# Attention and token/channel mixer on one core: a sixth pair of row tiles as block products, and two products of the last pair issued one slot earlier

## The chip, the cores and the metric

The kernel runs on one core of a Trainium2 chip. The metric is the time of one execution on the device in microseconds. Every engine of the core (PE for matrix products, DVE and POOL for elementwise work, ACT for activation functions, SP for most of the DMA issues) works through its own queue in order and waits on semaphores that the other engines raise.

## The reference

Twelve heads of cosine attention over 448 positions in a batch of 8, followed by a mixer: a two-layer product along the positions (448 to 256 to 448) with a residual, and a two-layer product along the channels (768 to 1536 to 768) with a residual.

```
q_n = q / (norm(q) + 1e-6);  k_n = k / (norm(k) + 1e-6)
attn = softmax(q_n @ k_n^T / tau)          # tau = 0.1
x = (attn @ v), heads side by side         # 8 x 448 x 768
u = x + (relu(x^T @ w_tok1) @ w_tok2)^T
out = u + relu(u @ w_ch1) @ w_ch2
```

Inputs and output are float32. The kernel's matrix products take float16.

## The kernel before, in words

**Slots.** The work is cut into 48 slots, one for each pair of heads of one batch element (6 pairs by 8 elements). The order of the instructions is written out by hand; no scheduler changes it. A slot i of the main loop (lines 1071 to 1134) issues, in this order on PE: three score products (`score`, tiles psS, 448 columns each), the product with V of the slot before (`pv_rest`, `pv`, tiles psO), a first piece of channel work, the last quarter of the scores (`score_rest`, psQ), the second position product of two slots before (`tok2`, psU), more channel work, and the first position product of the slot before (`tok1`, psR). ACT takes the exponential of each score tile; DVE divides the PV result by the row sums (`rec` and `x`, lines 405 and 406) and adds the residual (`u`, line 455). `side(i)` issues what prepares later slots: POOL casts V, squares and scales q and k (lines 242, 264, 316, 324), DVE sums the squares (line 280), ACT and DVE make the inverse norms, SP issues the transposes by DMA and the loads. `ACT_SQ` and `ACT_K` say in which slots ACT does the squares instead of POOL.

**Channel work.** Batch element b has 12 first-layer units (`ch1(b, ct)`: six products of 448 columns, ACT writes the result after a ReLU into the tile gt) and seven half row tiles per two elements in the second layer (`ch2`: 12 products of 384 columns, DVE adds u). gt holds two elements at a time, one for even b and one for odd b, so an element's units may only be written when the row tiles of the element two before have been read. The table `WORK` deals these units out over the slots.

**Pairs of row tiles as block products.** Two row tiles r1, r2 of 128 rows can be computed together with seven block products (Strassen's scheme in Winograd's form) of six matmuls each, where the direct way takes eight such groups. The pairs stand in the list `G`. `sg_sum(1..4)` are the four sums of the input, on POOL, into the three tiles sg0 to sg2; `fast_weights2` made the sums of the weights earlier. `sg_first` (one slot) issues products 1 and 2 (`head`), 6 (`middle`) and 7 (`end`); `sg_second` (another slot) issues 5 and 4 (`head`) and 3 (`end`). DVE adds the parts up into two output tiles `osg` (lines 690 and 696; all of DVE's and POOL's elementwise sums are recorded at line 544). A row tile with m = 3 has 64 rows of one batch element and 64 of the next, so its residual is added in two instructions of 64 rows. `FIRST` and `SECOND` give the slots. In `sg_second`, product 3 adds into the same PSUM tile psZ that product 5 began, so that the tile stays occupied between them.

**PSUM.** There are eight banks: a pool `ps` of two single banks (tag "b") and a pool `ps2` of three double banks (tag "s"). Scores, psQ, psY and psZ take turns in the three of `ps2`; psO, psU, psR, psX and psW in the two of `ps`. A product into a bank waits until the engine that reads the earlier tile there has done so.

**The tail.** Batch elements 6 and 7 are computed after slot 47 with the same seven-product scheme in both layers (`p1` to `p7` for the first, `q1` to `q7` for the second). The sums of the first layer's weights are `fast_weights1(1..4)`: number 1 on POOL (tile s1w), number 2 on DVE (s2w, from s1w), number 4 on POOL (s4w, from s2w), number 3 on DVE (in place in wc1t). `fast_x` are the sums of the first layer's input (t1x to t4x), `fast_g(0, k)` the sums of the second layer's input for the first tail pair (s1g, s2g). `upose` turns the residual stream by PE (psT) for the last two slots.

What sets the order around the change is this loop body and the lines that follow it:

```
            if i == NP_ALL - 1:
                fast_weights1(2, nc.vector)
            side(i)
            if i == NP_ALL - 2:
                cast_v(i + 1)
                fast_weights1(1, nc.gpsimd)
```

Of the kernel before, what the change touches and what calls it, by code (L numbers as in the profile page):

```python
# [7 lines left out]
FP32 = mybir.dt.float32  # L8
# [14 lines left out]
def kernel(  # L23
# [12 lines left out]
    nc = tc.nc  # L36

    B, H, S, E = q.shape
    D = H * E
# [7 lines left out]
    DH = 384  # L47
    NPAIR = H // 2
    NP_ALL = B * NPAIR
# [42 lines left out]
    ps2 = ctx.enter_context(tc.tile_pool(name="ps2", bufs=3, space=bass.MemoryType.PSUM))  # L92
# [442 lines left out]
    def ch2(b, m, n):  # L535
        lo, hi, st = CUTS[n]
        return lambda wide: m_ch2(b, m, lo, hi, st, wide)
# [22 lines left out]
    def fast_weights1(n, eng):  # L560
        s, w = fw["s"], w1part
        out, a, b, op = {1: (s[0], w(1, 0), w(1, 1), ALU.add), 2: (s[1], s[0], w(0, 0), ALU.subtract),
                         3: (w(1, 0), w(0, 0), w(1, 0), ALU.subtract), 4: (s[2], w(0, 1), s[1], ALU.subtract)}[n]
        tt(eng, out if n == 3 else out[:], a[:] if n == 2 else a, b[:] if n == 4 else b, op)
# [52 lines left out]
    def p1(d):  # L617
        bank2("X", d)
        prod1(1, d, px, True)
        nc.scalar.activation(out=etile("e1", d), in_=px[d][:, :, 0:S], func=AF.Copy)  # L620
# [60 lines left out]
    def sg_prod(n, r1, r2, out, start=True):  # L681
        s1, s2, s3 = sgs
        a = {1: lambda: part(*r1, 0), 2: lambda: part(*r1, 1), 3: lambda: s2, 4: lambda: part(*r2, 1),
             5: lambda: s1, 6: lambda: s2, 7: lambda: s3}[n]()
        for j in range(HC):
            nc.tensor.matmul(out[:, 0:DH], a[:, j], fast_w2(n, j), start=(start and j == 0), stop=(j == HC - 1),  # L686
                             skip_group_check=True)

    def sg_add(out, src, other):
        tt(nc.vector, out, src[:, 0:DH], other, ALU.add)  # L690
# [14 lines left out]
    def sg_first(r1, r2):  # L705
        def head():
            st = slot_g[r1] = {}
            st["o"] = [outp.tile([128, D], FP32, name=f"osg_{r[0]}_{r[1]}", tag="ost") for r in (r1, r2)]
            y = st["y"] = ps2.tile([128, 512], FP32, name=f"psY_{r1[0]}_{r1[1]}", tag="s")
            o1 = st["o"][0]  # L710
            sg_prod(1, r1, r2, y)
            sg_add_u(o1[:, 0:DH], y, r1, 0)
            x = ps.tile([128, 512], FP32, name=f"psX_{r1[0]}_{r1[1]}", tag="b")
            sg_prod(2, r1, r2, x)
            sg_add(o1[:, 0:DH], x, o1[:, 0:DH])

        def middle():
            st = slot_g[r1]
            sg_prod(6, r1, r2, st["y"], False)
            sg_add_u(st["o"][0][:, DH:D], st["y"], r1, 1)  # L720

        def end():
            st = slot_g[r1]
            sg_prod(7, r1, r2, st["y"], False)
            for h in (1, 0):
                sg_add_u(st["o"][1][:, DH * h:DH * (h + 1)], st["y"], r2, h)

        return head, middle, end

    def sg_second(r1, r2):  # L730
        def head():
            st = slot_g[r1]
            z = st["z"] = ps2.tile([128, 512], FP32, name=f"psZ_{r1[0]}_{r1[1]}", tag="s")
            o2 = st["o"][1]
            sg_prod(5, r1, r2, z)
            sg_add(o2[:, DH:D], z, o2[:, DH:D])
            w = ps.tile([128, 512], FP32, name=f"psW_{r1[0]}_{r1[1]}", tag="b")
            sg_prod(4, r1, r2, w)
            sg_add(o2[:, 0:DH], w, o2[:, 0:DH])
            if r2[1] < 3:  # L740
                sg_store(r2, o2)
            else:
                for n in range(2):
                    (c, p0, p1), = pieces(384, S)
                    nc.sync.dma_start(out=out[r2[0] - 1 + n].rearrange("(p c) d -> c p d", c=NCH)[c, p0:p1],
                                      in_=o2[64 * n:64 * n + 64])

        def end():
            st = slot_g[r1]
            o1 = st["o"][0]  # L750
            sg_prod(3, r1, r2, st["z"], False)
            sg_add(o1[:, DH:D], st["z"], o1[:, DH:D])
            sg_store(r1, o1)

        return head, end
# [122 lines left out]
    def run(b, lo, hi):  # L878
        return [ch1(b, ct) for ct in range(lo, hi)]

    def halves(b, m):
        return [ch2(b, m, 0), ch2(b, m, 1)]

    G = [((1, 1), (1, 2)), ((2, 1), (2, 2)), ((3, 0), (3, 1)), ((4, 0), (4, 1)), ((4, 2), (5, 3))]
    WORK = {
        7: run(0, 0, 2), 8: run(0, 2, 5), 9: run(0, 5, 7), 10: run(0, 7, 10), 11: run(0, 10, 12),
        12: [ch2(0, 0, 0), ch2(0, 1, 0)], 13: [ch2(0, 2, 0)], 14: [ch2(0, 0, 1), ch2(0, 1, 1)],
        15: [ch2(0, 2, 1)] + run(1, 0, 2), 16: run(1, 2, 6), 17: run(1, 6, 9), 18: run(1, 9, 12),
        19: [ch2(1, 3, 0), ch2(1, 0, 0)], 20: [ch2(1, 3, 1), ch2(1, 0, 1)],
        21: run(2, 0, 3), 22: run(2, 3, 7), 23: run(2, 7, 10), 24: run(2, 10, 11), 25: run(2, 11, 12),  # L890
        26: halves(2, 0), 27: run(3, 0, 3), 28: run(3, 3, 4), 29: run(3, 4, 5),
        30: run(3, 5, 9), 31: run(3, 9, 12), 32: [ch2(3, 3, 0), ch2(3, 2, 0)], 33: [ch2(3, 3, 1), ch2(3, 2, 1)],
        34: run(4, 0, 1), 35: run(4, 1, 2), 36: run(4, 2, 5), 37: run(4, 5, 9), 38: run(4, 9, 12),
        39: run(5, 0, 3), 40: run(5, 3, 5), 41: run(5, 5, 6), 42: run(5, 6, 8), 43: run(5, 8, 10), 44: run(5, 10, 12),
        45: [], 46: [], 47: [],
    }
    FIRST = {24: G[0], 28: G[1], 34: G[2], 41: G[3], 46: G[4]}
    SECOND = {25: G[0], 29: G[1], 35: G[2], 45: G[3], 47: G[4]}
    SUMS = {}

    def sums_at(i, *what):
# [3 lines left out]
    for i in (13, 14, 14, 15, 16, 17, 18, 19, 19, 20, 20, 21):  # L905
        n, m = ws.pop(0)
        sums_at(i, lambda n=n, m=m: fast_weights2(n, m))
    for g, at in zip(G, ((22, 23, 24, 25), (26, 27, 28, 29), (32, 33, 34, 35), (39, 40, 41, 42), (46, 46, 45, 47))):
        for n in (3, 1, 2, 4) if g is G[4] else (1, 2, 3, 4):
            sums_at(at[n - 1], lambda n=n, g=g: sg_sum(n, *g))  # L910
    ACT_K = (14, 19, 20)

    LATE = NP_ALL - 10
    ACT_SQ = range(2 * NPAIR + 1, NP_ALL - 5)
# [1 line left out]
    with tc.manual_schedule():  # L916
# [102 lines left out]
        i = NPAIR  # L1019
# [51 lines left out]
        for i in range(NPAIR + 1, NP_ALL):  # L1071
            b, pj = i // NPAIR, i % NPAIR
            for c in range(KC):
                score(i, c)
                if c == 1 and NPAIR + 2 <= i < NP_ALL - 2:
                    norms(i + 2)
            if i == NPAIR + 1:
                upose(i - 4, 2)
                tok2(i - 2, pe=True)
                pv_wide(i - 1)  # L1080
                upose_act(i - 2)
                x_wide(i - 1)
                sums(i + 2)
            else:
                pv_rest(i - 1)
                pv(i - 1, 0)
                pv(i - 1, 1)
            if i == NP_ALL - 1:
                fast_weights1(2, nc.vector)
            side(i)  # L1090
            if i == NP_ALL - 2:
                cast_v(i + 1)
                fast_weights1(1, nc.gpsimd)
            todo = WORK[i]
            first = sg_first(*FIRST[i]) if i in FIRST else None
            second = sg_second(*SECOND[i]) if i in SECOND else None
            if first or second:
                (first or second)[0]()
            elif todo:
                todo.pop(0)(True)  # L1100
            if old(i):
                score(i, KC)
            else:
                score_rest(i)
            if i in ACT_SQ:
                square(i + 3, 1, act=True)
            if first:
                first[1]()
            if i > NPAIR + 1:
                tok2(i - 2)  # L1110
            if i + 1 < DMA_T0:
                tpose(i + 1)
            if first:
                tok1(i - 1)
                first[2]()
            elif todo and not second:
                todo.pop(0)(True)
            for fn in todo:
                fn(False)
            if second:  # L1120
                second[1]()
            if not first:
                tok1(i - 1)
            if i + 3 < NP_ALL:
                sums(i + 3)
            if i == NP_ALL - 3:
                early.close()
                tail = ctx.enter_context(tc.tile_pool(name="tail", bufs=1, side="right", reuse_waits="tile"))
                tail_tiles()
            if i == NP_ALL - 2:  # L1130
                fast_g(0, 1)
                fast_g(0, 2)
            if i == NP_ALL - 1:
                fast_weights1(4, nc.gpsimd)
        last = NP_ALL - 1
        fw["room"] = {}
        p1(0)
        pv_rest(last)
        pv(last, 0)
        pv(last, 1)  # L1140
# [2 lines left out]
        for k in (3, 4):  # L1143
            fw["t"][k] = xtile(k, "x", [128, HD, S])
        gts["new"] = tail2.tile([128, CT, 512], FP16, name="gt_new")
        fast_weights1(3, nc.vector)
        p1(1)
        fast_x(1, 0, HD)
# [128 lines left out]
```

## Time and profile before

| | us |
|---|---|
| median of 3 runs | 378.64 |
| lowest, highest | 378.26, 380.29 |
| profiled execution | 377.93 |
| its span, first to last instruction | 376.1 |
| PE busy | 360.6 |
| DVE busy | 260.5 |
| ACT busy | 251.5 |
| POOL busy | 293.4 |

The profiled execution's own time is 1.8 us longer than its span, and 0.7 us under the median of the runs. In the profile, a line such as L686 is the line of kernel.py that recorded an instruction; `psY<-tw,sg` names what it writes and reads; an idle time in brackets is that of the engine just before the instruction, with the one that ended it. The granted clock of PE was 0.997 over the span. Slots are cut at the start of the first score product (L363) of each; slot 12 starts at 71.5 us, slot 33 at 213.0, slot 47 at 301.4.

### The profile page before, as it was taken

The numbers are of one execution on the slowest core, as the hardware profiler recorded it, in microseconds if no ns is written. First come the engines' busy times: TensorE is split into PE (matmuls) and PEld (weight loads), VectorE is DVE, ScalarE is ACT, GpSimd is POOL, SyncE is SP. The second block draws the span as 40 slices with busy tenths as digits, with TensorE's granted clock in tenths as the row PEclk, the third lists the DMA queues.
The fourth block names the chain that finished last, engine by engine and source line by source line (L and its number), as shares of the span: only waits on it lengthen the run. The fifth ranks groups of instructions, "written<-read, shape, count | busy, mean of one in ns | idle before, by whom it ended". The sixth has DMA issues, their size and how long they took to land.

```text
span 376.1 us, 10388 instructions
## 1 busy us (share of the span) xinstructions
PE 360.6 (96%) x4060; PEld 236.0 (63%) x4060; DVE 260.5 (69%) x589; ACT 251.5 (67%) x440; POOL 293.4 (78%) x405
## 2 busy tenths in 40 slices
PE   6788999999999999999999999999999969999995
PEld 5566666676666766666666766666666646556663
DVE  7789765776556763875864876646777698786873
ACT  5999887857788597666677755978688434265110
POOL 8899998989989987878766887469989962345753
PEclk9999999999999999999999999999999999999998
DMA  7999999988989798879898979979875713103344
GB/s 200 270 254 197 265 255 205 208 149 163 231 206 198 163 246 173 178 171 237 163 204 187 162 182 214 225 172 182 196 148 124 150 40 99 22 3 91 89 125 126
DMA packets 118224, 64.64 MB, mean 172 GB/s; under 512 B 74272, under 2 KB 114848, under 8 KB 118176
## 3 DMA queue, kind: packets, MB, share of 16 engines
q1 hardware_dynamic: 111984, 58.25, 71.1%
q0 software_dynamic: 5616, 5.21, 8.8%
q8 instruction: 31, 0.51, 0.6%
q10 hardware_dynamic: 576, 0.52, 0.5%
q14 instruction: 17, 0.14, 0.1%
HBM read 43.45 MB, written 11.01 MB: 145 GB/s over the span
## 4 chain that ended last, share of the span: by engine, by line
PE 86%; DVE 5%; ACT 5%; DMA 1%; issue 1%; POOL 0%; SPq 0%; DVEq 0%; ACTq 0%
PE psG L483 22%; PE psO L402 9%; PE psF L500 8%; PE psS L363 8%; PE psU L452 5%; PE psR L438 5%; PE psYo L790 4%; PE psY L686 3%; ACT pt L364 3%; PE psY L598 3%; PE psXo L790 3%; PE psZo L790 3%; PE psZ L686 2%; PE psZ L598 2%; PE psX L598 2%; PE psQ L370 2%
## 5 line engine op out<-in xcount | busy, mean ns | idle before, releaser
L364 ACT ACTIVATE pt<-psS 128x896 f16<-128x896 f32 (+1 forms) x156 | 135.7, 911 | 28.3 <-PE psS L363 28.2
L483 PE MATMUL psG<-ut,wc1t 128*128 128x448 f16 x432 | 90.1, 352 | 0.0
L316 POOL TENSOR_TENSOR kq<-kf,rn 128x384 f16<-128x384 f32 (+1 forms) x43 | 38.0, 885 | 35.0 <-DVE rn L293 34.2
L483 PEld LDWEIGHTS <-wc1t 128*128 128x128 f16 x432 | 40.4, 97 | 32.0
L486 ACT ACTIVATE gt<-psG 128x448 f16<-128x448 f32 x72 | 38.9, 541 | 30.6 <-PE psG L483 30.6
L280 DVE TENSOR_REDUCE ssq<-sq 128x15 f32<-128x960 f32 (+2 forms) x45 | 49.9, 1111 | 2.9 <-ACT sq L262 2.9
L441 DVE TENSOR_SCALAR rt<-psR 128x256 f16<-128x256 f32 x48 | 20.1, 418 | 43.6 <-PE psR L438 43.6
L363 PE MATMUL psS<-qk 64*128 64x448 f16 x312 | 41.2, 354 | 4.4 <-DVE qk L342 3.0
L316 POOL TENSOR_TENSOR kq<-qf,rn 112x512 f16<-112x512 f32 x41 | 42.8, 1044 | 2.8
L455 DVE TENSOR_TENSOR u<-psU,x 128x512 f16<-128x512 f32 x48 | 33.1, 689 | 12.4 <-PE psU L452 11.4
L402 PE MATMUL psO<-vt,pt 128*128 128x65 f16 (+1 forms) x1024 | 39.2, 194 | 0.0
L406 DVE TENSOR_TENSOR x<-psO,rec 128x256 f16<-128x256 f32 x82 | 34.8, 424 | 2.8
L402 PEld LDWEIGHTS <-pt 128*128 128x128 f16 (+1 forms) x1024 | 34.2, 97 | 3.5 <-issue 0.9
L500 PE MATMUL psF<-wc2t,gt 128*128 128x384 f16 x192 | 33.8, 326 | 0.0
L264 POOL TENSOR_TENSOR sq<-kf 128x384 f32<-128x384 f32 (+1 forms) x35 | 30.0, 857 | 0.1
L452 PE MATMUL psU<-rt,w2t 128*128 128x128 f16 x384 | 29.4, 220 | 0.6 <-POOL w2t L211 0.6
L452 PEld LDWEIGHTS <-w2t 128*128 128x128 f16 x384 | 24.8, 98 | 8.0 <-DVE rn L293 0.8
L438 PEld LDWEIGHTS <-w1t 128*128 128x128 f16 x384 | 24.8, 98 | 7.9 <-issue 2.1
L438 PE MATMUL psR<-x,w1t 128*128 128x128 f16 x384 | 29.3, 219 | 0.2 <-DVE u L455 0.2
L371 ACT ACTIVATE pt<-psQ 128x448 f16<-128x448 f32 x36 | 19.6, 544 | 12.3 <-PE psQ L370 12.2
L324 POOL TENSOR_SCALAR kq<-kr,rn 64x64 f16<-64x64 f32 x72 | 22.7, 315 | 3.6
L363 PEld LDWEIGHTS <-qk 64*128 64x128 f16 x312 | 12.6, 94 | 19.0 <-issue 6.3
(164 smaller groups left out, 654.5 us busy)
## 6 DMA issues: line engine op xcount, KB each, us to landing
qf<-in_q_dram SPq DMA_DIRECT2D x43, 224.0 KB, 3.9
vf<-in_v_dram SPq DMA_DIRECT2D x36, 192.0 KB, 3.6
kf<-in_k_dram SPq DMA_DIRECT2D x34, 192.0 KB, 3.7
wc1t<-in_moe_w_ch_dram POOLq DMA_DIRECT2D x4, 576.0 KB, 10.5
wc2t<-in_moe_w_ch_dram POOLq DMA_DIRECT2D x2, 1152.0 KB, 12.7
kf<-in_k_dram SPq DMA_DIRECT2D x9, 224.0 KB, 8.4
vf<-in_v_dram SPq DMA_DIRECT2D x9, 224.0 KB, 8.3
kr<-in_k_dram SPq DMA_DIRECT2D x24, 48.0 KB, 3.6
```

Of the source, the lines that this page charges most:

```text
L280: nc.vector.tensor_reduce(out=st["ssq"][0:n, sl], in_=st["sq"][0:n, sl], axis=AXX.X, op=ALU.add)
L316: eng.tensor_tensor(out=kq[0:p, a, 0:n].rearrange("p c g e -> p g c e"), in0=st["kq"[a]][:].rearrange("p (g c) e -> p g c e", g=2), in1=_b ...
L363: nc.tensor.matmul(psS[:, hh, 0:S], qk[hb, c * n:c * n + 128], qm[hb], start=True, stop=True)
L364: nc.scalar.activation(out=pts[i % 2][0:n, 2 * S * c:2 * S * (c + 1)].rearrange("p (h s) -> p h s", h=2), in_=psS[0:n, :, 0:S], func=AF.Ex ...
L402: nc.tensor.matmul(psO[:, m, 0:E + 1], pts[i % 2][0:n, at:at + 128], vt[0:n, i % HP, nch * hh + c, 0:E + 1], start=(old(i) and c == 0), st ...
L406: nc.vector.tensor_tensor(out=st["x"][:, :, hh * E:(hh + 1) * E], in0=psO[:, :, 0:E], in1=_bcast_free(rec[:], E), op=ALU.mult)
L438: nc.tensor.matmul(psR[:, tt], w1t[:, w1[m], tt * 128:(tt + 1) * 128], st["x"][:, m], start=(m == 0), stop=(m == 3))
L452: nc.tensor.matmul(psU[:, m], w2t[:, tt, lo:lo + 128], st["rt"][:, tt], start=(tt == 0), stop=(tt == TT - 1))
L483: nc.tensor.matmul(psG[:, 0:S], wc1t[:, dt, ct * 128:(ct + 1) * 128], ut[b][:, dt].rearrange("p m s -> p (m s)")[:, lo:lo + S], start=(dt ...
L486: nc.scalar.activation(out=gt[:, ct, (b % 2) * S:(b % 2 + 1) * S], in_=psG[:, 0:S], func=AF.Relu)
L500: nc.tensor.matmul(psF[:, 0:hi - lo], gt[:, ct, at:at + 128], wc2t[:, ct, lo:hi], start=(ct == 0), stop=(ct == CT - 1))
L790: nc.tensor.matmul(out[:, o:o + hi - lo], a[:, j], fast_w2(n, j)[:, lo:hi], start=(start and j == 0), stop=(j == HC - 1), skip_group_check ...
```

## The change

- A sixth pair ((2, 0), (3, 3)) joins `G`. These two row tiles are no longer done by `ch2`. Its sums 1 and 2 stand in slot 32, sum 3 in slot 33, sum 4 in slot 34.
- The first-layer units of batch elements 2, 3 and 4 are dealt out anew over slots 21 to 38. The first pair's second half moves from slot 25 to 26, the third pair from slots 34 and 35 to 37 and 38. The sums of the second and third pair move with them, the second pair's in the order 3, 1, 2, 4.
- For the sixth pair and for the last one (`AHEAD`), products 5 and 4 follow product 7 in the first slot (33 and 46). DVE then adds product 5 into both output tiles at once, and product 3, in the second slot, gets a PSUM tile of its own (psV).
- In slot 32 the square of k goes to ACT.
- `fast_weights1(1)` moves from slot 46 to slot 47 on POOL, behind the last pair's sum 4. `fast_weights1(2)` moves on DVE from slot 47 to behind the last product with V, and `fast_weights1(4)` on POOL follows it there.
- `fast_g(0, 1)` and `fast_g(0, 2)` on DVE move from the end of slot 46 to slot 47 behind product 3; `p1(0)` moves with them, ahead of `tok1` of slot 46.

```
-    def sg_second(r1, r2):
+    def sg_second(r1, r2, split=False):
         def head():
...
             sg_prod(5, r1, r2, z)
             sg_add(o2[:, DH:D], z, o2[:, DH:D])
+            if split:
+                o1 = st["o"][0]
+                sg_add(o1[:, DH:D], z, o1[:, DH:D])
+                del st["z"]
...
-            sg_prod(3, r1, r2, st["z"], False)
-            sg_add(o1[:, DH:D], st["z"], o1[:, DH:D])
+            z = ps2.tile([128, 512], FP32, name=f"psV_{r1[0]}_{r1[1]}", tag="s") if split else st["z"]
+            sg_prod(3, r1, r2, z, split)
+            sg_add(o1[:, DH:D], z, o1[:, DH:D])
...
-    G = [((1, 1), (1, 2)), ((2, 1), (2, 2)), ((3, 0), (3, 1)), ((4, 0), (4, 1)), ((4, 2), (5, 3))]
+    G = [((1, 1), (1, 2)), ((2, 1), (2, 2)), ((3, 0), (3, 1)), ((4, 0), (4, 1)), ((4, 2), (5, 3)), ((2, 0), (3, 3))]
...
-        21: run(2, 0, 3), 22: run(2, 3, 7), 23: run(2, 7, 10), 24: run(2, 10, 11), 25: run(2, 11, 12),
-        26: halves(2, 0), 27: run(3, 0, 3), 28: run(3, 3, 4), 29: run(3, 4, 5),
-        30: run(3, 5, 9), 31: run(3, 9, 12), 32: [ch2(3, 3, 0), ch2(3, 2, 0)], 33: [ch2(3, 3, 1), ch2(3, 2, 1)],
-        34: run(4, 0, 1), 35: run(4, 1, 2), 36: run(4, 2, 5), 37: run(4, 5, 9), 38: run(4, 9, 12),
+        21: run(2, 0, 3), 22: run(2, 3, 6), 23: run(2, 6, 8), 24: run(2, 8, 9), 25: run(2, 9, 12),
+        26: run(3, 0, 1), 27: run(3, 1, 4), 28: run(3, 4, 5), 29: run(3, 5, 6),
+        30: run(3, 6, 9), 31: run(3, 9, 12), 32: halves(3, 2), 33: [],
+        34: run(4, 0, 2), 35: run(4, 2, 5), 36: run(4, 5, 8), 37: run(4, 8, 10), 38: run(4, 10, 12),
...
-    FIRST = {24: G[0], 28: G[1], 34: G[2], 41: G[3], 46: G[4]}
-    SECOND = {25: G[0], 29: G[1], 35: G[2], 45: G[3], 47: G[4]}
+    FIRST = {24: G[0], 28: G[1], 33: G[5], 37: G[2], 41: G[3], 46: G[4]}
+    SECOND = {26: G[0], 29: G[1], 34: G[5], 38: G[2], 45: G[3], 47: G[4]}
...
-            if i == NP_ALL - 1:
-                fast_weights1(2, nc.vector)
             side(i)
             if i == NP_ALL - 2:
                 cast_v(i + 1)
+            if i == NP_ALL - 1:
                 fast_weights1(1, nc.gpsimd)
...
             if first:
                 tok1(i - 1)
                 first[2]()
+                if ahead:
+                    sg_second(*first[3], True)[0]()
...
             if second:
                 second[1]()
+            if i == NP_ALL - 1:
+                fast_g(0, 1)
+                fast_g(0, 2)
+                p1(0)
             if not first:
                 tok1(i - 1)
...
-            if i == NP_ALL - 2:
-                fast_g(0, 1)
-                fast_g(0, 2)
-            if i == NP_ALL - 1:
-                fast_weights1(4, nc.gpsimd)
         last = NP_ALL - 1
         fw["room"] = {}
-        p1(0)
...
         gts["new"] = tail2.tile([128, CT, 512], FP16, name="gt_new")
+        fast_weights1(2, nc.vector)
+        fast_weights1(4, nc.gpsimd)
         fast_weights1(3, nc.vector)
         p1(1)
```

## The prediction

> **What bounds the kernel now.** I read the page first: PE is busy for 96% of the span and carries 86% of the chain that ended last, so a time changes by what PE issues and by what it waits for.
>
> ```profile
> span 376.1 us, 10388 instructions
> PE 360.6 (96%) x4060; PEld 236.0 (63%) x4060; DVE 260.5 (69%) x589; ACT 251.5 (67%) x440; POOL 293.4 (78%) x405
> ```
>
> Next the waits of PE alone. All others lie in the first 72 us; these three (of the psS line the 0.8) fall into slot 47, the last attention step.
>
> ```profile
> PE psW L686 <- DVE x L406: 1.6, 1, 1.6
> PE psS L363 <- ACT pt L364: 1.0, 2, 0.8
> PE psZ L686 <- DVE osg L544: 0.5, 1, 0.5
> ```
>
> Then the windows view, for slots 13 to 45 in one stretch and for slot 47 up to the tail's first product. Column one is the length, column two PE's busy time. Over 33 slots PE has no gap: there a slot lasts as long as PE's issue, and a wait added there is lost in full. Slot 47 has 2.9 us of gaps.
>
> ```profile
> 78.77:294.51 215.74, 215.70 (x2515) 141.92 (x2513) 142.47 (x348) 160.40 (x294) 176.86 (x265) 1.00 0.88 187
> 301.41:310.38 8.97, 6.07 (x74) 3.95 (x74) 8.49 (x15) 3.08 (x4) 5.40 (x3) 1.00 0.11 28
> ```
>
> PE's timeline there (start, length, then idle before and its releaser):
>
> ```profile
> 301.41 0.55 PE L363 MATMUL psS<-qk 64*128 64x448 f16 x4
> 302.79 0.36 PE L363 MATMUL psS<-qk 64*128 64x448 f16 x2 [0.82 <-ACT pt L364]
> 306.69 1.15 PE L686 MATMUL psW<-tw,gt 128*128 128x384 f16 x6 [1.59 <-DVE x L406]
> 308.96 1.14 PE L686 MATMUL psZ<-wc2t,sg 128*128 128x384 f16 x6 [0.49 <-DVE osg L544]
> ```
>
> Last, POOL and DVE around it. Two things matter: where POOL's long sums of weights stand, and that s1g took 1.56 us where its twin of the same shape took 0.55.
>
> ```profile
> 303.31 1.64 POOL L544 TENSOR_TENSOR sg<-gt,sg 128x768 f16<-128x768 f16 x1
> 308.52 4.55 POOL L544 TENSOR_TENSOR s4w<-wc1t,s2w 128x2304 f16<-128x2304 f16 x1 [3.57 <-DVE s2w L544]
> ```
> ```profile
> 303.81 1.56 DVE L544 TENSOR_TENSOR s1g<-gt 128x768 f16<-128x768 f16 x1
> 307.09 1.35 DVE L544 TENSOR_TENSOR s2w<-s1w,wc1t 128x2304 f16<-128x2304 f16 x1
> 313.53 1.35 DVE L544 TENSOR_TENSOR wc1t<-wc1t 128x2304 f16<-128x2304 f16 x1
> 314.80 0.85 DVE L544 TENSOR_TENSOR t1x<-ut,ut 128x1344 f16<-128x1344 f16 x1
> 316.50 0.38 DVE L544 TENSOR_TENSOR t2x<-ut,t1x 128x448 f16<-128x448 f16 x1
> 332.72 0.55 DVE L544 TENSOR_TENSOR room<-gt 128x768 f16<-128x768 f16 x1
> ...
> 342.74 0.71 DVE L544 TENSOR_TENSOR t2g<-t1g,gt 128x768 f16<-128x768 f16 x1
> 343.84 0.88 DVE L544 TENSOR_TENSOR t3g<-gt 128x768 f16<-128x768 f16 x1
> ```
> ```profile
> 340.93 2.10 POOL L544 TENSOR_TENSOR f<-f,u 128x384 f32<-128x384 f32 x2 [1.10 <-DVE f L544]
> 343.12 1.19 POOL L544 TENSOR_TENSOR orow<-f,f 128x384 f32<-128x384 f32 x1
> ```
>
> s1g (two SBUF inputs) started inside POOL's sum, which ended at 304.95; s1g ended at 305.37, 0.42 later. In the tail's second layer t2g and t3g end at 343.45 and 344.72, again 0.42 and 0.41 after the POOL instruction that ran when they started (343.03, 344.31). DVE sums with one input in PSUM kept their 0.55 us under POOL work. So a DVE sum of two SBUF tiles does not advance while a POOL sum runs. Before, s4w ran at 308.52 to 313.07, beside DVE work from PSUM only, and wc1t started at 313.53.
>
> **The change part by part.**
>
> 1. *Sixth pair.* 4 second-layer units (48 matmuls of 384 columns) become 7 products (42): 6 x 0.1625 (0.975 per product of six in the chain) = **-0.97 us** on PE. First-layer units stay 36, only dealt out anew; 1.14 us each wherever they stand. Where slots 22 to 38 become shorter or longer, the cover is checked on POOL, the fullest engine there: a slot costs it 0.50 cast, 1.12 square, 2.6 scaling, one sum 1.64, together 5.9, plus 0.35 every third slot. The shortest (slot 23, two units, 5.1) is followed by 7.8; slot 40 has the same shape before and PE has no gap at 41. Slot 32 gets two sums, and its key square goes to ACT (4.02 of 6.63 us busy); POOL's scaling there ends about 0.9 us later, for a transpose that is used two slots on. Cost zero. In slot 28 sum 2 now stands in the slot whose P6 reads it: POOL ends it about 2.6 us into the slot, P6 comes at 3.5. SP's queue: as many stores as before, two slots' worth moved by one slot, loads behind them run five slots ahead. Zero.
>
> 2. *P5, P4 drawn ahead in slot 33.* psZ is now emptied by two DVE sums at once, and the second row of the pair is a split tile (four 64-row sums, 2.26 us at 301.52). After P7 DVE has 4 sums of psY, 2 of psZ (0.55, one every 0.47), 1 of psW. Counting from the moment PE has issued P7, DVE starts at 0.20 (301.52 against 301.32): psY is free at 2.46, psZ at 3.50, psW at 3.97. PE ends P5 and P4 at 1.95; its second score needs psY's bank, its third psZ's, and the first PV matmul of the second head psW's. Without waits PV starts at 2.6, with them at 4.0: **+1.4 us** in slot 34, which had no gap. Behind these sums DVE's L280 waits, and ACT's Ln behind that; both end before PE needs them (third exponential at 6.4, P3 at 7.9).
>
> 3. *Slot 46 to 47, the same order.* Again from P7 (301.32 before). On PE the timeline has PV at 1.0 us, psQ 0.19, U and R 0.45 each, P3 0.975, a first-layer product of the tail 1.14, psT 0.22; DVE's first x is ready 1.45 us after PV starts, its second 0.55 later; u takes 0.69, rt 0.41. PV at 4.0 as above, ends 4.97; psQ 5.16; U waits for x (5.42), 5.48 to 5.93; P3 to 6.90; p1(0) to 8.04; tok1 to 8.49. s1g and s2g run at 7.6 to 8.7 with POOL idle (s1w now follows the sum and ends at 4.5), so 0.55 each. rt is ready at 9.2 and PV of 47 waits for its bank: 9.2 against 10.29 (311.61) before, **-1.1**. The three old waits are gone, 0.3, 0.8, 0.3, 0.3 and 0.6 stand in their place.
>
> 4. *Weight sums behind the last PV.* Now s2w, then wc1t, t1x, u, rt, t2x, t3x, t4x are DVE's order, and POOL's s4w starts when s2w ends. DVE: x ends 11.2, s2w 12.45, wc1t 13.7. PE: PV 10.2, p1(1), p2(0), U, R, p2(1) to 14.46, then psT needs u, which stands behind t1x. s4w asks at 12.5, during wc1t. What the trace doesn't show is who goes next at 13.7.
>  - s4w first: 13.7 to 18.3, t1x ends at 19.0, u 19.6, psT 19.7 (PE stands 5.2 us); the rest of the chain (p1(2), U, p5, psT, p2(2)) brings p6(0) to 24.3, against 19.87 (321.19) before: +4.4.
>  - t1x first: u 15.1, psT 15.2; s4w 14.5 to 19.1, t2x stands until 19.35, the second u is ready at 22.05 and psT waits from 18.1 to 22.1: p6(0) at 23.5, +3.6.
>  - no blocking at all: u 15.1, second u 18.5, p6(0) at 19.9: 0.0.
>  I take s4w first, since it asks 1.1 us before t1x; +4.4 (the -1.1 of step 3 is in it). After p6 the order is the old one, PE without gaps.
>
> [...]
>
> Sum: -0.97 + 1.4 + 4.4 = +4.8 us. It is made against the profiled execution (span 376.1, 377.93 in all), which lies 0.7 under the median; put on the median 378.64: **383.4 us**, 1.3% slower. With t1x first 382.7.
>
> **The rivals.**
>
> - *The clock falls in the stall.* The mean granted clock is 0.94 in the window 372 to 374 and 0.72 in 372 to 376, so it falls to 0.5 at 373.8, 2.3 us after the last matmul ended (371.45); a stall of 4 to 5 us is longer. At the start, matmuls of 128 columns stood 0.107 us apart (12 in 2.00 to 3.00) until 5.1 and 0.056 after (8 in 5.2 to 5.6), some 3.5 us at half speed. Twice that loss here: 3.5 x 0.5 less the slack before the second psT: +1.6, **385.0**. Against it: gaps of up to 1.6 us left the clock at 1.00, and the tail's fall came after more idle time than one such gap. [...]
> - *POOL's long sum lets DVE through.* The rows show blocking under POOL sums of up to 1.64 us, none under 4.55. If s4w yields between parts, step 4 gives 0.0: -0.97 + 1.4 + 0 = **379.1**, no measurable difference. It decides if psT in the tail waits for u less than 1.9 us.
> - *Only the old gaps go.* If the sums behind P7 hide under PE, 2.9 us of waits and 0.97 us of products go: **374.8**. Against it: seven DVE sums of 3.8 us behind 1.95 us of PE, with banks named by the program.
>
> **How the numbers follow.** Chances: forecast (either order) 0.45, clock also falls 0.32, no blocking 0.15, only gaps go 0.05, something slower still 0.03. Range 379.0 to 385.4: from the no-blocking case to the clock's fall with s4w first. The likeliest alone: 382.6 to 383.5. Faster and slower count from 0.5% (1.9 us), about what a measurement of this kernel can tell from no change: slower 0.80, same 0.15, faster 0.05.
>
> **What would show it.** Step 1: 4054 matmuls, no PE gap in slots 21 to 33. Step 2: in slot 34 PE waits for osg on DVE, some 0.8 us before psS and 0.3 before psO. Step 3: s1g at 0.55. Step 4: one of wc1t, t1x, t2x over 4 us on DVE, and PE idle 4 to 5 us before psT on DVE u. Wrong would make it: s4w beside DVE sums of normal length, or PE reaching the psY bank after DVE has emptied it.

## The result and the profile after

The changed kernel takes 390.61 us (median of 6 runs, 388.18 to 391.52). The kernel before took 379.22 us on the same chip. The ratio is 1.0295, 95% interval 1.0249 to 1.0341; it is taken over the fast runs, which leaves out one slow run of the kernel before. It is slower by some 11 us, where 4.8 were forecast. The profiled execution took 391.45 us, with a span of 389.6.

The head of the page, with the row of the clock that PE was granted (40 slices of 9.7 us):

```profile
span 389.6 us, 10394 instructions
...
PE 366.4 (94%) x4054; PEld 238.5 (61%) x4054; DVE 267.5 (69%) x595; ACT 252.6 (65%) x442; POOL 299.8 (77%) x407
...
PEclk9999999999999999978999999999999998999999
```

PE is busy for 366.4 us, 5.8 more than before, though it issues six matmuls fewer (4054). In two places the clock is not full. The waits of PE alone (total, times, longest); those that lie in the first 72 us are left out:

```profile
PE psT L468 <- DVE u L455: 4.8, 1, 4.8
PE psG L483 <- DMA ut<-u: 3.3, 1, 3.3
...
PE psS L363 <- DVE osg L544: 1.4, 2, 0.7
...
PE psS L363 <- DMA qk<-kq: 0.9, 2, 0.6
...
PE psO L385 <- DVE rt L441: 0.4, 1, 0.4
```

The second line was not in the prediction. The first two lines as they stand in PE's timeline (start, length, idle before and its releaser), with the five products ahead of the first stall:

```profile
168.17 1.11 PE L483 MATMUL psG<-ut,wc1t 128*128 128x448 f16 x5
172.60 0.53 PE L483 MATMUL psG<-ut,wc1t 128*128 128x448 f16 x1 [3.32 <-DMA ut<-u]
...
329.05 0.50 PE L468 MATMUL psT<-id,u 128*128 128x128 f16 x3 [4.85 <-DVE u L455]
```

The windows view of PE around the two stalls (length, busy times of PE, PE's weight loads, DVE, ACT and POOL, then the granted clock). In slot 26, PE stands from 169.28 to 172.60. The clock is halved from 171.36 until 178.18, which reaches 2.3 us into slot 27 (175.83 to 183.00). It is halved a second time from 328.37 to 331.78:

```profile
165.00:171.30 6.30, 4.27 (x45) 2.65 (x42) 3.50 (x10) 3.27 (x7) 5.62 (x9) 1.00 0.97 157
171.40:178.10 6.70, 5.50 (x44) 3.29 (x44) 2.04 (x3) 2.21 (x4) 1.63 (x2) 0.50 1.07 262
328.40:331.70 3.30, 2.65 (x11) 1.30 (x12) 3.15 (x9) 0.00 (x0) 0.00 (x0) 0.50 0.00 0
```

By stretches, cut at the first score product of a slot; "p6(0)" is the tail's first product 6. The last column is a run that is told of below, in which two edits remove the stalls; the last row ends at the start of the last matmul:

| stretch (us) | before | after | both stalls removed |
|---|---|---|---|
| start to slot 21 | 130.3 | 131.7 | 130.6 |
| slots 21 to 25 | 34.7 | 32.1 | 32.1 |
| slots 26, 27 | 12.9 | 19.1 | 13.0 |
| slots 28 to 32 | 35.1 | 33.9 | 33.9 |
| slots 33 to 38 | 41.4 | 45.6 | 45.6 |
| slots 39 to 45 | 40.2 | 40.2 | 40.2 |
| slot 46 to p6(0) | 26.7 | 32.0 | 26.6 |
| p6(0) to the last matmul | 50.0 | 50.0 | 50.0 |

Units and pairs have moved between the rows from 21 to 38, so only their sum compares: 124.0 before and 130.8 after. The 1.4 us ahead of slot 21 lie in code that is the same in both kernels; the profiles below lie between 130.2 and 133.0 us there, with no relation to their edits. What is left is 6.8 us in slots 21 to 38, 6.1 of it in slots 26 and 27 (19.1 against the last column's 13.0), and 5.3 us between slot 46 and p6(0).

What happened in slot 26 is read from SP's issues in the changed kernel:

```profile
160.16 0.60 SPq L135 DMA_DIRECT2D vf<-in_v_dram  x1
160.81 1.25 SPq L143 DMA_DIRECT2D vr<-in_v_dram  x2
162.16 1.23 SPq L461 DMA_TRANSPOSE ut<-u  x1
163.51 1.24 SPq L348 DMA_TRANSPOSE qk<-kq  x1
164.84 0.53 SPq L153 DMA_DIRECT2D qf<-in_q_dram  x1
165.43 0.46 SPq L135 DMA_DIRECT2D kf<-in_k_dram  x1
165.93 0.46 SPq L135 DMA_DIRECT2D vf<-in_v_dram  x1
166.49 1.19 SPq L461 DMA_TRANSPOSE ut<-u  x1
```

The transposed residual of pair 23 (u, written by DVE until 161.82) is issued at 166.49. It stands behind the transposing DMA of slot 27's q and k, which waits for POOL's scaling (until 163.43), and behind three loads, and it lands only at 172.6. First-layer unit (3,0) reads all six pairs of batch element 3, of which this is the last. The change draws that unit in slot 26, where PE reaches the last of its six products at 169.28. Before, the unit stood in slot 27, where PE began it at 173.23 and its sixth product at about 174.2 (0.19 us apart), and did not wait. The two rows of the trace of before:

```profile
167.85 2.19 SPq L461 DMA_TRANSPOSE ut<-u  x1
...
173.23 1.29 PE L483 MATMUL psG<-ut,wc1t 128*128 128x448 f16 x6
```

The tail, DVE and then POOL:

```profile
317.18 0.55 DVE L544 TENSOR_TENSOR s1g<-gt 128x768 f16<-128x768 f16 x1
317.76 0.56 DVE L544 TENSOR_TENSOR s2g<-s1g,gt 128x768 f16<-128x768 f16 x1
...
320.67 1.35 DVE L544 TENSOR_TENSOR s2w<-s1w,wc1t 128x2304 f16<-128x2304 f16 x1
321.93 1.35 DVE L544 TENSOR_TENSOR wc1t<-wc1t 128x2304 f16<-128x2304 f16 x1
323.20 5.19 DVE L544 TENSOR_TENSOR t1x<-ut,ut 128x1344 f16<-128x1344 f16 x1
```

```profile
322.10 5.58 POOL L544 TENSOR_TENSOR s4w<-wc1t,s2w 128x2304 f16<-128x2304 f16 x1 [7.96 <-DVE s2w L544]
```

s4w's record begins at 322.10, while wc1t runs (until 323.28), and is 5.58 us long where it was 4.55 before. t1x, 0.85 us before, takes 5.19. u stands behind it, and psT waits for u.

### The profile page after: what moved, and what is told of

The parts are those of the page before. It is cut to its first block, busy times and chain, and to the rows that moved or that the text cites. A ratio compares the mean times of both kernels' runs of the same rounds, so it can differ in the third digit from the quotient of the medians.

```text
span 389.6 us, 10394 instructions
## 1 busy us (share of the span) xinstructions
PE 366.4 (94%) x4054; PEld 238.5 (61%) x4054; DVE 267.5 (69%) x595; ACT 252.6 (65%) x442; POOL 299.8 (77%) x407
## 4 chain that ended last, share of the span: by engine, by line
PE 75%; DMA 8%; DVE 8%; POOL 3%; ACT 2%; issue 2%; SPq 0%; DVEq 0%; POOLq 0%
PE psG L483 19%; PE psO L402 8%; PE psS L363 7%; PE psF L500 5%; PE psU L452 5%; PE psR L438 4%; PE psY L686 4%; DMA kf<-in_k_dram 4%; PE psYo L795 4%; PE psY L598 3%; PE psZo L795 3%; PE psXo L795 3%; DMA qk<-kq 2%; PE psZ L686 2%; DVE ssq L280 2%
## 5 line engine op out<-in xcount | busy, mean ns | idle before, releaser
L486 ACT ACTIVATE gt<-psG 128x448 f16<-128x448 f32 x72 | 39.0, 542 | 33.9 <-PE psG L483 33.9
L483 PEld LDWEIGHTS <-wc1t 128*128 128x128 f16 x432 | 40.2, 97 | 31.6
L363 PE MATMUL psS<-qk 64*128 64x448 f16 x312 | 42.8, 361 | 6.0 <-DVE qk L342 2.8
L438 PEld LDWEIGHTS <-w1t 128*128 128x128 f16 x384 | 25.1, 99 | 8.0 <-issue 2.5
L264 POOL TENSOR_TENSOR sq<-kf 128x384 f32<-128x384 f32 (+1 forms) x34 | 29.2, 858 | 0.7 <-DMA kf<-in_k_dram 0.7
L500 PE MATMUL psF<-wc2t,gt 128*128 128x384 f16 x144 | 25.3, 326 | 0.0
```

The lines of the kernel that those rows point to most:

```text
L363: nc.tensor.matmul(psS[:, hh, 0:S], qk[hb, c * n:c * n + 128], qm[hb], start=True, stop=True)
L438: nc.tensor.matmul(psR[:, tt], w1t[:, w1[m], tt * 128:(tt + 1) * 128], st["x"][:, m], start=(m == 0), stop=(m == 3))
L483: nc.tensor.matmul(psG[:, 0:S], wc1t[:, dt, ct * 128:(ct + 1) * 128], ut[b][:, dt].rearrange("p m s -> p (m s)")[:, lo:lo + S], start=(dt ...
L486: nc.scalar.activation(out=gt[:, ct, (b % 2) * S:(b % 2 + 1) * S], in_=psG[:, 0:S], func=AF.Relu)
L500: nc.tensor.matmul(psF[:, 0:hi - lo], gt[:, ct, at:at + 128], wc2t[:, ct, lo:hi], start=(ct == 0), stop=(ct == CT - 1))
```

## The experiments

Ratios are to the kernel before, run on the same chip between them. "Under the changed kernel" is worked out from the ratio: 0.01 is 3.8 us.

**The unit back in slot 27.**

```
-        26: run(3, 0, 1), 27: run(3, 1, 4), 28: run(3, 4, 5), 29: run(3, 5, 6),
+        26: [], 27: run(3, 0, 4), 28: run(3, 4, 5), 29: run(3, 5, 6),
```

> The changed kernel with one edit: first-layer unit (3,0), which it draws in slot 26, is drawn in slot 27 again, with the three units after it. Theory A (the unit is too early for its own operand: the transposing DMA for pair 23 was issued on SP at 166.49 and PE waited 3.3 us for it, and the 6.8 us of clock at 0.5 that followed came out of this stall): the wait ahead of psG in slot 26 goes, the clock does not fall near 171, slots 26 and 27 together take about 13.5 to 14 us instead of 19.1, and the time is 5 to 6 us under the changed kernel's, about 385. Theory B (POOL and SP lag behind in slots 22 to 26 because of the new dealing as a whole): the wait is met again one slot later, and the time is within 1 us of the changed kernel's.

Measured: 386.1 us, ratio 1.0181 (1.0106 to 1.0256), 4.3 us under the changed kernel. Slots 26 and 27 took 13.6 us rather than 19.1, and the clock stayed at 1.00 there. PE's waits, the first in the tail and the second in slot 27:

```profile
PE psT L468 <- DVE u L455: 4.9, 1, 4.9
...
PE psG L483 <- DMA ut<-u: 0.5, 1, 0.5
```

Theory A, with less of a gain than its 5 to 6 us; with four runs the interval only just touches that of the changed kernel (1.0256 and 1.0249). Even in slot 27 the unit waits 0.5 us: the new dealing brings PE to its sixth product at 171.05 rather than 174.2.

**The same unit moved in the kernel before.**

```
-        26: halves(2, 0), 27: run(3, 0, 3), 28: run(3, 3, 4), 29: run(3, 4, 5),
+        26: halves(2, 0) + run(3, 0, 1), 27: run(3, 1, 3), 28: run(3, 3, 4), 29: run(3, 4, 5),
```

> The kernel before with one edit: the first first-layer unit of slot 27, (3,0), is drawn at the end of slot 26; nothing else changes, and the count of instructions stays. Theory A (it is this move that costs the 3.3 us wait ahead of psG, by the landing of the transposed pair 23, which the kernel before issued at 167.85 and had at about 173): PE waits 2 to 5 us ahead of psG in slot 26; if the clock falls behind the wait as it did in the changed kernel, the time is 4 to 6 us over the kernel before, if it does not, 2 to 3.5 us. Theory B (the wait in the changed kernel comes of its other moves): no wait over 0.5 us and the time stays within 0.5 us.

Measured: 380.51 us, ratio 1.0019 (0.9987 to 1.0051), which can't be told from the kernel before.

```profile
PE psG L483 <- DMA ut<-u: 0.9, 1, 0.9
```

Neither theory: the move alone costs a wait of 0.9 us in the profile. PE reaches the sixth product at 172.15, 2 us earlier than before, and the transposed pair lands at 173.03. In the four profiles of the changed dealing with the unit in slot 26, PE reaches it at 168.2 to 169.4 and the pair lands at 170.5 to 172.6, so the waits are 3.3, 2.3, 1.7 and 2.6 us. The new dealing moves the first pair's second half from slot 25 to slot 26, in place of the two half row tiles there: slots 21 to 25 take 32.1 to 32.8 us in these profiles rather than 34.7, and 12 matmuls of 384 columns stand ahead of the unit in slot 26 rather than 24. (The units taken out of slots 22 and 23 come back in slot 25.) So PE arrives another 2.7 to 4.0 us earlier, while the DMA comes only 0.4 to 2.5 us earlier. It is the two together that make the stall.

**The loads behind the transposing DMA.** Is it the queue, or the transfer itself?

```
-            if i + 6 < NP_ALL and i + 2 >= DMA_T0:
+            if i + 6 < NP_ALL and i + 2 >= DMA_T0 and i != 25:
                 load_qk(i + 6)
+            if i == 25:
+                return
...
             if i > NPAIR + 1:
                 tok2(i - 2)
+            if i == 25:
+                load_qk(i + 6)
+                load_v(i + 3)
```

> The changed kernel with one edit: in slot 25 the three loads of pairs 28 and 31 are issued on SP behind the transposing DMA of pair 23 rather than ahead of it. Theory A (SP's queue is what is late: in the changed kernel u of pair 23 stood at 161.8 and its DMA was issued at 166.49, behind the transposing DMA of pair 27 at 163.51 and three loads): it is issued about 1.6 us sooner in relation to the end of the transposing DMA ahead of it, lands 1 to 2 us sooner, the wait ahead of psG in slot 26 falls by 1 to 2 us from what it was in the runs of the same dealing (1.7 to 3.3 us), the clock does not fall there, and the time is 1.5 to 4.5 us under the changed kernel's. Theory B (the transfer itself is slow there, whatever stands ahead of it in the queue): it lands at the same place in slot 26 within 0.5 us, and the time does not move by more than 1 us.

Measured: 385.77 us, ratio 1.0177 (1.0148 to 1.0207), 4.5 us under the changed kernel. SP's issues:

```profile
161.38 1.23 SPq L461 DMA_TRANSPOSE ut<-u  x1
162.72 1.24 SPq L348 DMA_TRANSPOSE qk<-kq  x1
164.06 1.25 SPq L461 DMA_TRANSPOSE ut<-u  x1
165.40 0.53 SPq L153 DMA_DIRECT2D qf<-in_q_dram  x1
165.99 1.45 SPq L135 DMA_DIRECT2D kf<-in_k_dram  x1
```

u's DMA follows 1.34 us behind the start of the one ahead of it, where it was 2.98. The sixth product starts at 168.20, 0.1 us later than the five ahead of it alone would have it, which fits a landing some 4.1 us behind the issue, only just in time. Slots 26 and 27 take 13.3 us, and the clock stays at 1.00 there. Theory A: three loads that nobody needs for three slots and more, standing ahead of one small DMA, cost 4.5 us. The edit that gives the unit back to slot 27 gains no more.

**s4w on DVE.**

```
-        fast_weights1(4, nc.gpsimd)
         fast_weights1(3, nc.vector)
...
         fast_x(3, 2, 3)
+        fast_weights1(4, nc.vector)
```

> The changed kernel with one edit: the weight sum s4w, 5.58 us on POOL right behind the last pair of block products, is computed on DVE after the last first-layer activation sum. Theory A (the POOL sum keeps the 0.85 us sum t1x on DVE from ending for 5.19 us, and psT waits for it): t1x takes about 0.9 us, the wait of 4.85 us ahead of psT falls to between 0 and 0.7, the clock does not fall near 328, and the time is 4.5 to 6.5 us under the changed kernel's. Theory B (DVE is late in the tail from the reordered work in slot 47, whatever POOL does): t1x still ends near 328 and the time falls by under 1 us.

Measured: 382.98 us, ratio 1.0079 (1.0045 to 1.0113), 8.2 us under the changed kernel. DVE in the tail, and PE's waits:

```profile
316.15 1.35 DVE L544 TENSOR_TENSOR s2w<-s1w,wc1t 128x2304 f16<-128x2304 f16 x1
317.42 1.35 DVE L544 TENSOR_TENSOR wc1t<-wc1t 128x2304 f16<-128x2304 f16 x1
318.68 0.85 DVE L544 TENSOR_TENSOR t1x<-ut,ut 128x1344 f16<-128x1344 f16 x1
...
324.90 1.35 DVE L544 TENSOR_TENSOR s4w<-wc1t,s2w 128x2304 f16<-128x2304 f16 x1
```

```profile
PE psG L483 <- DMA ut<-u: 2.3, 1, 2.3
...
PE psT L468 <- DVE u L455: 0.5, 1, 0.5
```

Theory A. t1x takes 0.85 us again and slot 46 to p6(0) 26.6 us, 5.4 less than in the changed kernel. s4w itself costs DVE 1.35 us where nobody waits for it. The gain is 1.7 us more than the most expected. In the profile the rest lies in slot 26, which waited 2.3 us here and kept its clock (1.00 from 164 to 178 us); the timed runs beside it have no trace, so for them this is not shown.

**s4w in three parts on POOL.**

```
+        if n == 4:
+            for j in range(HD):
+                tt(eng, out[:, j], a[:, j], b[:, j], op)
+            return
```

> The changed kernel with one edit: the weight sum s4w on POOL is made in three instructions of 768 columns rather than one of 2304. Theory A (DVE's sum t1x is held while one POOL sum runs, and gets its turn between two): t1x takes 1 to 3 us rather than 5.19, the wait of 4.85 us ahead of psT falls to 0.5 to 2.7 us, the clock does not fall near 328, and the time is 2 to 5.5 us under the changed kernel's. Theory B (POOL keeps DVE out for all three): t1x stays over 4.5 us and the time within 1 us.

Measured: 387.91 us, ratio 1.025 (1.0205 to 1.0294), 1.7 us under the changed kernel; slot 46 to p6(0) took 30.0 us, 2.0 less than in the changed kernel. The intervals of the two ratios overlap, so by the times alone the gain isn't shown. POOL, then DVE beside it:

```profile
319.04 6.63 POOL L544 TENSOR_TENSOR s4w<-wc1t,s2w 128x768 f16<-128x768 f16 x3 [7.98 <-DVE s2w L544]
```

```profile
320.14 2.29 DVE L544 TENSOR_TENSOR t1x<-ut,ut 128x1344 f16<-128x1344 f16 x1
...
323.29 0.89 DVE L544 TENSOR_TENSOR t2x<-ut,t1x 128x448 f16<-128x448 f16 x1
324.10 1.82 DVE L544 TENSOR_TENSOR t3x<-ut 128x448 f16<-128x448 f16 x1
325.84 0.38 DVE L544 TENSOR_TENSOR t4x<-ut,t2x 128x448 f16<-128x448 f16 x1
```

Theory A: beside POOL's three parts (6.63 us together), t1x takes 2.29 us rather than 5.19. But t2x and t3x take 0.89 and 1.82 us where they took 0.38 in the kernel before: by these lengths, an estimate, each of the three parts holds one DVE sum. PE waits for u twice, 2.3 us in all and 2.0 at the longest, and the clock falls all the same: its mean from 325 to 334 us is 0.87. So the gain lies below the range given.

**The sixth pair not drawn ahead.**

```
-    AHEAD = (G[4], G[5])
+    AHEAD = (G[4],)
```

> The changed kernel with one edit: the sixth pair (slots 33 and 34) is not drawn ahead; its P5 and P4 stand in slot 34 as those of the first four pairs do. Theory A (drawing ahead costs slot 34 its two waits for DVE's osg and brings nothing back): the gaps of 0.12 and 0.68 us in slot 34 go and the time is 1.3 us under the changed kernel's. Theory B (the waits only move, since the DVE is the one behind): the gaps of slot 34 stay within 0.3 us of their sum and the time changes by under 0.5 us.

Measured: 389.52 us, ratio 1.0257 (1.0197 to 1.0318), which can't be told from the changed kernel. So the slots decide. PE in slot 34:

```profile
220.48 0.37 PE L363 MATMUL psS<-qk 64*128 64x448 f16 x2 [0.82 <-ACT pt L364]
...
223.38 1.15 PE L686 MATMUL psW<-tw,gt 128*128 128x384 f16 x6 [0.59 <-DVE x L406]
```

Both theories were wrong. The two waits for osg go, and two others of 0.82 and 0.59 us come. Slots 33 and 34 took 16.5 us, against 16.0 drawn ahead. The pattern is that of slot 47 in the kernel before, where psS and psW waited in the same places. Drawing ahead lowers the waits from 1.4 to 0.8 us. The pairs in slots 24, 28 and 34 of the kernel before have their second half in the next slot too, and no wait there. Two things set the sixth and the last pair apart: no first-layer unit stands behind product 7 in slots 33 and 46, and one of their row tiles is split into 64 and 64 rows. No run here shows which of the two it is, or what another spacing would do.

**Both stalls removed**: the edits of the first and the fourth experiment together.

> The changed kernel with the edits of the two runs before together: first-layer unit (3,0) back in slot 27, and s4w on DVE after the last first-layer activation sum. Theory A (the excess over the kernel before is these two stalls with the clock that falls in them, and 0.8 us from slot 34 and the rest of the unit's wait): the clock does not fall before the last slice, slots 21 to 38 take about 124.8 us against 124.0 of the kernel before, slot 46 to the first P6 about 26.6 against 26.7, and the time is within 1.2 us of the kernel before, at a ratio of 1.000 to 1.004. Theory B (the two stalls hide a third delay, which shows when they are gone): a new wait of over 1 us and a ratio of 1.006 or more.

Measured: 379.72 us, ratio 1.0016 (0.9994 to 1.0038). PE's waits behind the first 72 us are these:

```profile
PE psS L363 <- DVE osg L544: 1.4, 2, 0.7
...
PE psT L468 <- DVE u L455: 0.5, 1, 0.5
PE psO L385 <- DVE rt L441: 0.4, 1, 0.4
...
PE psS L363 <- DMA qk<-kq: 0.3, 1, 0.3
```

Theory A: the ratio falls from 1.0295 to 1.0016, and in the profile the clock is 1.00 over the span. The stretches are in the table above. Slots 21 to 38 take 124.6 us against 124.0. What remains of the change is worth nothing that can be measured.

**A version that beats both.** The stall of 1.59 us in slot 47 of the kernel before came from DVE, which computed s1g and s2g there beside POOL's sums. They are needed only in the second layer of the tail:

```
             if i == NP_ALL - 2:
-                fast_g(0, 1)
-                fast_g(0, 2)
...
         fast_x(4, 2, 3, nc.gpsimd)
+        fast_g(0, 1, nc.gpsimd)
+        fast_g(0, 2, nc.gpsimd)
```

> The kernel before with one edit: the last two block-product activation sums of the last four row tiles (DVE, at the end of slot 46) are computed on POOL behind its last first-layer activation sum. Theory A (in slot 47 PE waits 0.82, 1.59 and 0.49 us for DVE, which these sums keep busy): the three waits, 2.9 us in all, fall to under 1.2, and the time is 1.5 to 2.2 us under the kernel before, at a ratio of 0.994 to 0.996. Theory B (what is late then is the POOL sum or what waits for it): a wait of over 1 us ahead of the first P7 or of P6, and the time is the same or longer.

Measured: 376.55 us, ratio 0.9949 (0.992 to 0.9978), 1.9 us faster than the kernel before. POOL's queue in the tail:

```profile
321.88 1.03 POOL L544 TENSOR_TENSOR t4x<-ut,t2x 128x448 f16<-128x448 f16 x1 [8.27 <-DVE t2x L544]
322.87 1.64 POOL L544 TENSOR_TENSOR s1g<-gt 128x768 f16<-128x768 f16 x1
324.58 1.65 POOL L544 TENSOR_TENSOR s2g<-s1g,gt 128x768 f16<-128x768 f16 x1
```

```profile
PE psS L363 <- ACT pt L364: 1.0, 2, 0.8
```

Theory A: two of the three waits of slot 47 are gone (the 0.8 for ACT stays), and slot 46 to p6(0) takes 24.5 us rather than 26.7. The two sums now stand where POOL was idle, and DVE's sums beside them read PSUM and keep their length (e<-psY,e, two in 2.26 us in both kernels). The profiled execution is the second slowest of the nine (378.74 us): it took 2.7 us more than the kernel before ahead of slot 21, where nothing was edited. Slot 47 gets rid of its waits for DVE in this way without a weight sum being moved to where DVE adds SBUF tiles on the way to PE.

## Why the prediction was wrong

The direction stood, and so did the sizes of three of its four steps. The forecast of +4.8 us was 6 to 7 us short.

- **Step 1 failed**, at "1.14 us each wherever they stand" and at "SP's queue ... Zero". The step counted stores and loads on SP, but not the transposing DMA of u that stands behind them, nor when the unit that reads it is reached. The trace of before had what was needed: this DMA issued at 167.85, and a median of 3.8 us from issue to landing of these DMAs, so a landing near 171.7 (by the profiles it was up to 173), with the unit's sixth product at 174.2. The unit's move takes 2 us from that distance and the lighter slots ahead of it, 21 to 26, another 2.7 to 4.0. Runs: waits of 1.7 to 3.3 us, and in the profile of the changed kernel a clock halved for 6.8 us behind the longest of them; taking the unit back, or issuing the DMA ahead of the loads, gains 4.3 and 4.5 us. The sum of the pair's products (4054 matmuls, -0.97) was right in its count.
- **The cover of slot 23** was costed at zero, too. It takes 5.5 us instead of 5.1: PE waits 0.34 us for the transposing DMA of slot 24's q and k. In the six other profiles with this dealing the wait was 0.28 to 0.99 us, but for one (the unit back in slot 27), which had none and took 5.1.
- **Step 2 stood, as a cost of the changed kernel.** In slot 34, waits of 0.12 and 0.69 us for osg before psS and 0.09 before psO were found (0.8 and 0.3 were forecast), and the second head's product with V went on 4.04 us after PE had issued P7 (223.50 to 227.54), as forecast (4.0). The sum of steps 1 and 2 was +0.4, where 0.6 was measured with both stalls removed. But drawing ahead is not what makes the pair cost; plain, slots 33 and 34 take 0.5 us more.
- **Step 3 stood.** The product with V of slot 47 went on behind its wait 9.23 us after PE had issued P7 (309.54 to 318.77), as forecast (9.2). s1g took 0.55 us, with waits of 0.13, 0.68, 0.18 and 0.38 us in place of the three old ones (0.3, 0.8, 0.3, 0.3 and 0.6 forecast).
- **Step 4 stood**, with s4w first: t1x 5.19 us (the rows of before showed a hold under POOL sums of up to 1.64 us only), PE idle for 4.85 us ahead of psT (5.2 forecast), p6(0) 25.1 us after P7 (24.3 forecast, 25.9 with the clock's fall). Without this hold the stretch is as long as before (26.6 against 26.7 us), as the price of "no blocking at all", 0.0, said.
- **The first rival, that the clock falls in the stall, was true and had a chance of 0.32 only.** The clock fell behind this stall in the four profiles that have it in full (0.50 from 328.4 to 331.7 in the changed kernel, 0.57, 0.57 and 0.58 over 4 to 5 us in the others). They took 5.3 to 6.0 us more than the kernel before from slot 46 to p6(0); 4.4 were forecast without the fall, 6.0 with it. A second fall, behind slot 26, comes on top.

The sum by the runs, against the ratio's 11 us: tail 5.3 to 6.0, steps 1 and 2 without the stall 0.6 (the profile with both stalls removed, slot 23's wait of 0.32 in it), slots 26 and 27 2.0 to 6.1 (the four profiles of this dealing, over the 13.0 us with the stalls removed), together 7.9 to 12.7. Only one of these four, that of the changed kernel itself, lost its clock behind slot 26 (1.00 in the others, up to 178 or 180 us); how many of the timed executions did is not shown, since they have no trace. What sets the landing of that one DMA, between 4.4 and 6.1 us behind its issue, stays open.

## What to carry to other kernels

Before a consumer is moved to an earlier slot, look up in the trace when its last operand lands, and who stands ahead of it in the DMA queue; a slot that gets shorter moves every later consumer towards that landing. A long POOL sum should not start where DVE is about to add two SBUF tiles on the way to PE: an instruction of 4.55 us stretched a sum of 0.85 us to 5.19, and took 1.35 us on DVE itself. Price a stall of PE like these with the clock that may fall behind it: it fell behind stalls of 3.32 and 4.85 us, and in one run with waits of 2.3 us in all, and not behind stalls of 2.3 and 2.6 us elsewhere.

## What the runs showed of the hardware that was not expected

**The length of a stall alone does not tell whether the clock falls.** In the changed kernel the clock went to half at 171.36, 2.08 us after PE came to stand in the stall of 3.32 us, and at 328.37, 4.17 us after it came to stand in that of 4.85 us. It was full again 6.83 and 3.41 us later (178.18 and 331.78). The times between these four changes, 6.83, 150.19 and 3.41 us, are 2, 44 and 1 times 3.413 us. In the kernel before the clock stayed at 1.00 behind the wait of 1.59 us in slot 47 and fell at 373.78, 2.33 us after the last matmul's end. The stalls of 2.3 us (s4w on DVE) and 2.6 us (s4w in three parts) in slot 26 left the clock at 1.00, from 164 to 178 and from 164 to 180 us. In the tail of the run with three parts, PE waited for u twice, 2.0 us at the longest, and the mean clock from 325 to 334 us was 0.87. What decides between a wait that loses the clock and a longer one that does not is not shown.

**A POOL sum that began during one DVE sum ended ahead of the next.** s4w's record begins at 322.10, inside wc1t (until 323.28), and is 5.58 us long instead of 4.55; by that difference it contains a wait of some 1.0 us, an estimate. t1x, which stood next on DVE, started at 323.20 and ended at 328.39, 0.71 us after s4w's end at 327.68. In the run with three parts, POOL's 6.63 us and DVE's 2.29, 0.89 and 1.82 us, of sums that take 0.85, 0.38 and 0.38 in the kernel before, agree with the two taking turns by instruction, which is an estimate from these lengths.
